# First batch of a fused attention and MoE kernel: the last 64 rows of k, v and phi as one 128-partition transfer each

## The chip, the core and the metric

The kernel runs on one core of one Trainium2 chip. The metric is the device time of one execution in microseconds (us): 696.65 us is the median of three runs before the change (696.21 to 697.31). Engines are named as the profile names them: PE multiplies matrices (PEld loads its stationary operand), DVE is the vector engine, ACT the scalar engine, POOL the general-purpose engine, SP the sync engine, which issues most transfers. SPq and ACTq are the two queues on which transfers are issued; 16 DMA engines, shared by both queues, move the bytes.

## What is computed

```python
a = exp(phi - max(phi, axis=2)); a = a / (sum(a, axis=2) + 1e-9)      # over 32 memory slots
k_m = einsum('bhsm,bhsd->bhmd', a, k); v_m = einsum('bhsm,bhsd->bhmd', a, v)
scores = q @ k_m.T / sqrt(64)
attn = softmax(scores); out = attn @ v_m                              # per head
x = out.transpose(0, 2, 1, 3).reshape(4608, 512)
h = relu(x @ w_in); return (h * h) @ w_out                            # 512 -> 2048 -> 512
```

There are 8 batches, 8 heads, 576 positions, 64 values per head and 32 memory slots; everything is float32. The sequence of 576 positions is four full chunks of 128 rows and a last one of 64 rows. The sum over slots in `a` is divided out after the products over positions have been made.

## The kernel before, in words

The heads go in two *quads* of four heads. For one batch, `e_sb` holds phi with positions on the partitions: five chunks of 128 x 256 values, where the first 128 columns are quad 0 and the last 128 quad 1. `exp_phi` takes the largest value over the five chunks (`phi_mx`, lines 186 and 189), turns that with PE (206), reduces it (209), broadcasts it with PE (214), adds it on DVE (224) and exponentiates on ACT (225), chunk by chunk. `memories` then makes, chunk by chunk and quad by quad, the sums of the exponentials (`add`, line 318) and their products with k and v (`product`, line 327); between chunk 1 and chunk 2, after the sums of chunk 2, two dummy products stand (line 341). Lines 382 to 391 and 417 divide, turn and store the memories (`mem`). `attend` makes scores from q and `mem` (439) and the softmax on DVE and ACT (466 to 493). `decode` (lines 584 to 609) turns the 64-bit words in which the weights arrive into float32, partly on ACT, partly on DVE, last on POOL or DVE. Then follow the two MoE products, which fill the rest of the time.

What runs ahead of the steady stage is written out by hand. `loads` is the list of transfers in order; the first 12 entries are issued before any computation of the program is written, the others after it. `order` is the list in which the steps of the first batch are written, and so the order in which each engine's own instructions stand:

```python
order = (
    "e e e e e m d0 m m d0 m d1 a0 a0 a0 d0 a0 d1 d2 d1 a0 d2 u0 s a1 u0 d2 a0 o0 m o0"
)
```

Here `e` is a step of `exp_phi`, `m` of `memories`, `d0`, `d1` and `d2` of decoding w_in, `a0` and `a1` of `attend`, `u0` of the product of w_in with the memories, `o0` of decoding w_out. So the first DVE step of `d0` (lines 594 and 597) stands on DVE ahead of the copy that stores `mem` (line 417).

Transfers take eight semaphores in turn, in the order in which the program issues them on both queues together, and each transfer waits on its queue until the one eight places earlier has landed. The transfers of the first microseconds are: on ACTq the last 64 rows of phi (line 168), then three of quad 0's k and v (`u_hi`, `u_lo` at line 1316 with 256 rows each, `u_hi` at line 1320 with the last 64 rows); on SPq phi's chunks 0 and 1 (174), chunks 2 and 3 (176), three of quad 1's k and v (`wp` at 1316 twice and at 1320), then the first piece of w_in (565), q in two halves (428), and weights.

Of the kernel before, what the change touches and what calls it, by code (L numbers as in the profile page):

```python
# [9 lines left out]
F32 = mybir.dt.float32  # L10
# [17 lines left out]
def attn_moe_kernel(ctx: ExitStack, tc: tile.TileContext, qT, kv, phi, w_in, w_out, outT):  # L28
# [12 lines left out]
    nc = tc.nc  # L41
    ctx.enter_context(tc.manual_schedule())

    B, NQ, S = kv.shape[:3]
    P = 128
# [3 lines left out]
    D = 64  # L49
    M = 32  # L50
# [6 lines left out]
    CW = 2 * D + 2  # L57
    NCH = (S + P - 1) // P
# [9 lines left out]
    def rows(c):  # L68
        return min(P, S - c * P)

    const = ctx.enter_context(tc.tile_pool(name="const", bufs=1))
# [37 lines left out]
    e_sb = const.tile([P, NCH, NQ * P], F32, name="e_sb")  # L109
    kvb = [const.tile([P, 4, CW], F32, name=f"kvb{i}") for i in range(NCH)]  # L110

    def fill(c, t):
        if rows(c) < P:
            nc.gpsimd.memset(t[rows(c):], 0.0)
        if t.shape[-1] == CW:
            nc.gpsimd.memset(t[:rows(c), :, 2 * D:], 1.0)

    def fill_all():
        for c in range(NCH):
            fill(c, kvb[c])  # L120
            if rows(c) < P:
                nc.gpsimd.memset(e_sb[rows(c):, c], 0.0)

    ones = const.tile([P, CW - 2 * D], F32, name="ones")
    nc.gpsimd.memset(ones, 1.0)
# [35 lines left out]
    def load_phi(b, nc_q=nc.sync):  # L161
        nfull = S // P
        assert b == 0 or ("products", b - 1) in ready
        n = nfull if b else nfull // 2
        x = phi[b, :nfull * P].rearrange("(c p) x -> p c x", p=P)
        def short():
            if nfull < NCH:
                nc_q.dma_start(out=e_sb[:rows(nfull), nfull], in_=phi[b, nfull * P:])
                if b >= 3:
                    nc_q.dma_start(out=e_sb[P - rows(nfull):, nfull], in_=phi[b, nfull * P:])  # L170

        if not b:
            short()
        nc.sync.dma_start(out=e_sb[:, :n], in_=x[:, :n])
        if not b:
            nc.sync.dma_start(out=e_sb[:, n:nfull], in_=x[:, n:])
        if b:
            short()
        return [e_sb[:P if b >= 3 else rows(c), c] for c in range(NCH)]

    def chunk_max(e):

# [119 lines left out]
    def memories(b, e, kvs, mem):  # L302
# [9 lines left out]
        accs = [bank(ps, qd if not b or two else 0)[:, (qd if b and not two else 0) * CW:] for qd in range(NQ)]  # L312
        sums = [(ps_h.tile([P, 512], F32, name="h") if qd else tp) if not b else accs[qd][:, 2 * D:] for qd in range(NQ)]

        def add(qd, c):
            n = kvs[qd][c].shape[0]
            for j in range(4):
                nc.tensor.matmul(
                    sums[qd][M * j:M * (j + 1), :CW - 2 * D], e[c][:n, qd * P + M * j:qd * P + M * (j + 1)], ones[:n],
                    start=(c == 0), stop=(c == len(kvs[qd]) - 1),  # L320
                )

        def product(qd, c):
            y = kvs[qd][c]
            n, w = y.shape[0], y.shape[-1]
            for j in range(4):
                nc.tensor.matmul(  # L327
                    accs[qd][M * j:M * (j + 1), :w],
                    e[c][:n, qd * P + M * j:qd * P + M * (j + 1)],
                    y[:, j, :], start=(c == 0), stop=(c == len(kvs[qd]) - 1),  # L330
                )

        turns = range(NQ)
        if not b:
            for c in range(NCH):
                for qd in turns:
                    add(qd, c)
                if c == 2:
                    idle = new_ps(True)
                    for _ in range(2):  # L340
                        nc.tensor.matmul(
                            bank(idle, 0), ident, ident[:, None, :].broadcast_to([P, 4, P]), start=True, stop=True
                        )
                    done_ps(idle)
                for qd in turns:
                    product(qd, c)
        for qd in turns if b else ():
            if kvs[qd][0].shape[-1] < CW:
                for c in range(len(kvs[qd])):
                    add(qd, c)  # L350
            for c in range(NCH - 1 if two or whole else NCH):
                product(qd, c)
            if whole:
                for j in range(4):
                    nc.tensor.matmul(
                        accs[qd][M * j:M * (j + 1), :CW], e_sb[:, NCH - 1, qd * P + M * j:qd * P + M * (j + 1)],
                        kvb[NCH - 1][:, j, :], start=False, stop=True,
                    )
        if two:
            n = rows(NCH - 1)  # L360
            for j in range(4):
                for qd in range(NQ):
                    y = kvs[qd][-1] if qd else kvs[qd][-1][:n]
# [22 lines left out]
        for qd in turns:  # L386
            x = accs[qd][:, :2 * D].rearrange("p (x d) -> p x d", x=2)[:, :, None, :].broadcast_to([P, 2, 2, D])
# [9 lines left out]
        if b > 2:  # L397
            done_ps(ps)
            for j in range(4):
                if j == 2 or j and b > JOIN:  # L400
                    yield
                for k in range(2):
                    for x in range(2):
                        at = M * (2 * (j % 2) + k)
# [775 lines left out]
    def from_z(j, k, name, bufs):  # L1180

        x = work.tile([P, T], F32, name=name, bufs=bufs)
        (nc.vector.tensor_copy if late_on[f"z{k}"] >> pairs[j][1] & 1 else nc.scalar.copy)(x, banks["z"][:, :T])  # L1183
        return x
# [30 lines left out]
    def task_phi(b):  # L1215
        state[b]["phi"] = load_phi(b)
# [9 lines left out]
    def task_mem(b, kvs=None):  # L1226
        kvs = kvs or [state[b]["kv"][qd] for qd in range(NQ)]
        new_mem(b)
        return memories(b, [e_sb[:, c] for c in range(NCH)], kvs, state[b]["mem"])
# [68 lines left out]

    st = state[0]
    kvs = [None] * NQ  # L1300

    def first_kv(qd):

        if qd:
            x = [const.tile([P, 2, 2, 4, 2 * D], F32, name=f"wp{k}") for k in (2, 3)]
            rooms = [x[0][:, 0], x[0][:, 1], x[1][:, 0]]
        else:
            rooms = [const.tile([P, 2, 4, 2 * D], F32, name=n) for n in ("u_hi3", "u_lo3", "u_hi4")]
        queues = ((nc.scalar, nc.scalar, nc.scalar), (nc.sync, nc.sync, nc.sync))[qd]
        got = []  # L1310
        for t, nc_q in zip(rooms, queues):
            c = len(got)
            n = min(2, S // P - c)
            if n:
                x = kv[0, qd, c * P:(c + n) * P].rearrange("(c p) h x -> p c h x", p=P)
                nc_q.dma_start(out=t[:, :n], in_=x)
                got += [t[:, k] for k in range(n)]
            else:
                fill(c, t[:, 0])
                nc_q.dma_start(out=t[:rows(c), 0], in_=kv[0, qd, c * P:])  # L1320
                got.append(t[:, 0])
        kvs[qd] = got

    def first_phi():
        st["phi"] = load_phi(0, nc.scalar)
        fill_all()

    def next_kv():
        state[1]["kv"][1] = load_kv(1, 1, in_u())

    loads = [
        (first_phi,),
        (first_kv, 1),
        (fetch_w_in, 0, 0),
        (task_q, 0, 0),
        (fetch_w_in, 0, 1),
        (fetch_w_in, 1, 1),
        (fetch_w_in, 1, 0),
        (fetch_w_out, 0),
        (first_kv, 0),  # L1340
        (fetch_w_out, 1),
        (task_q, 0, 1),
# [215 lines left out]
    for k, step in enumerate(steps):  # L1558
        i, b, t, f = step
# [5 lines left out]
        n = f * P // FC  # L1565
# [53 lines left out]
    for j in range(-1, LAST + 1):  # L1619
# [31 lines left out]
        if new:  # L1651
            ffn1_product(u1, j + 1, 1, True)
            ffn1_product(z, j + 1, 2, True)
            x = from_z(j + 1, 2, *(("g_hi", 3) if old else ("r", 2)))
# [19 lines left out]
    n = (B - JOIN) * REST  # L1674
# [23 lines left out]
    last = banks["h"] + [banks["z"], banks["m"]]  # L1698
# [55 lines left out]
```

## Time and profile before

| | |
|---|---|
| median of three runs | 696.65 us |
| the profiled execution's own time | 695.58 us |
| its span, first to last instruction | 693.5 us |
| PE busy in the span | 682.5 us (98%) |
| PE busy in 0 to 45 us | 38.0 us of 45 |

The profiled execution is 1.07 us under the median, and 2.08 us of its time lie outside the span. PE busy in the first 45 us is the sum of nine stretches of 5 us. A busy PE is not PE at its peak, because matmuls are pipelined and dummy products count as busy. In the rows, "idle before <- X" is the time that an engine waited and what ended the wait; a wait for several semaphores is put down to the one that came last.

### The profile page before, as it was taken

How to read it: one execution, taken by the hardware profiler on the slowest of the kernel's cores; microseconds unless marked ns; L12 is line 12 of the kernel's file. 1: busy time of each engine (PE TensorE's matmuls, PEld its weight loads, DVE VectorE, ACT ScalarE, POOL GpSimd, SP SyncE). 2: the span in 40 equal slices, each digit the busy share in tenths (PEclk: the TensorE clock that was granted, in tenths of full speed). 3: DMA queues.
4: the chain of work that ended last, by engine and by line, in shares of the span. 5: the costliest groups of instructions: out<-in, count | busy, mean ns of one | idle time of the engine just before them, and what ended most of it. 6: DMA issues, size and time to landing. Idle time of an engine off the chain costs nothing.

```text
span 693.5 us, 14173 instructions
## 1 busy us (share of the span) xinstructions
PE 682.5 (98%) x5102; PEld 573.8 (83%) x5102; DVE 480.5 (69%) x1132; ACT 439.7 (63%) x1193; POOL 345.0 (50%) x528
## 2 busy tenths in 40 slices
PE   8899999999999999999999999999999999999997
PEld 4367889899998888888888888888888888888897
DVE  3879849455787976788678976788677765564432
ACT  3867798876456675566666665667666575655531
POOL 2200343343367675747575675757585567554200
PEclk9999999999999999999999999999999999999999
DMA  9997352509424642082336243355106110400102
GB/s 304 353 376 263 126 163 60 187 2 268 139 62 147 219 129 100 25 251 86 97 116 210 88 130 122 118 180 151 64 18 211 62 60 4 166 17 1 57 6 46
DMA packets 67846, 89.85 MB, mean 130 GB/s; under 512 B 6848, under 2 KB 56064, under 8 KB 64192
## 3 DMA queue, kind: packets, MB, share of 16 engines
q1 hardware_dynamic: 65888, 87.41, 38.9%
q10 hardware_dynamic: 1888, 1.54, 0.7%
q8 instruction: 40, 0.66, 0.4%
q14 instruction: 30, 0.25, 0.1%
HBM read 75.30 MB, written 13.63 MB: 128 GB/s over the span
## 4 chain that ended last, share of the span: by engine, by line
PE 91%; DMA 6%; DVE 2%; ACT 1%; issue 0%; ACTq 0%; SPq 0%; DVEq 0%
PE acc L1112 39%; PE h L1136 11%; PE acc L716 9%; PE z L1136 8%; PE h L687 6%; PE acc L708 4%; PE h L1704 2%; DMA e_sb<-in_phi 1%; DMA u_lo<-in_kv 1%; PE z L448 1%; PE m L1704 1%; PE z L1704 1%; PE ps_m L439 1%; PE m L327 1%; PE m L448 1%; DMA wp<-in_w_in 1%
## 5 line engine op out<-in xcount | busy, mean ns | idle before, releaser
L1112 PE MATMUL acc<-u_hi,wp 128*128 128x512 f32 x576 | 153.8, 396 | 0.0
L1112 PE MATMUL acc<-u_lo,wp 128*128 128x512 f32 x576 | 140.0, 392 | 0.0
L1112 PEld LDWEIGHTS acc<-u_hi,wp 128*128 128x128 f32 x576 | 101.2, 188 | 25.9 <-issue 11.0
L1112 PEld LDWEIGHTS acc<-u_lo,wp 128*128 128x128 f32 x576 | 105.5, 188 | 20.5
L1160 POOL TENSOR_TENSOR u_hi<-g_lo,u_hi 128x288 fp32r<-128x288 f32 (+1 forms) x76 | 59.2, 779 | 64.1 <-ACT g_lo L1157 44.2
L700 POOL TENSOR_TENSOR g_lo<-g,g_hi 128x288 fp32r<-128x288 f32 x48 | 43.2, 901 | 78.1 <-ACT g_hi L698 51.4
L1016 POOL TENSOR_TENSOR u_lo<-low,u_hi 128x128 fp32r<-128x128 f32 (+1 forms) x116 | 73.2, 636 | 16.6 <-ACT u_hi L1015 16.0
L1015 ACT CAST u_hi<-low 128x256 fp32r<-128x256 f32 (+1 forms) x160 | 52.8, 347 | 23.0 <-POOL low L1027 19.0
L1152 DVE CUSTOM_DVE_ANT_0 g_hi<-h,g_hi 128x288 f32<-128x288 f32 x95 | 42.7, 449 | 24.5 <-ACT g_hi L1183 24.2
L716 PE MATMUL acc<-g_hi,wp 128*128 128x288 f32 x360 | 58.8, 297 | 0.0
L1183 ACT COPY g_hi<-z 128x288 f32<-128x288 f32 x72 | 28.6, 398 | 44.2 <-PE z L1136 36.6
L716 PEld LDWEIGHTS acc<-g_hi,wp 128*128 128x128 f32 x360 | 51.0, 188 | 4.4 <-ACT r L689 1.7
L1155 ACT ACTIVATE u_hi<-g_hi 128x224 fp32r<-128x224 f32 x95 | 39.0, 410 | 21.7 <-DVE g_hi L1152 21.7
L1177 DVE TENSOR_TENSOR g_lo<-h,g 128x288 f32<-128x288 f32 x48 | 21.5, 448 | 34.9 <-ACT g L1173 33.8
L689 ACT ACTIVATE r<-h 128x288 f32<-128x288 f32 x64 | 26.0, 406 | 27.9 <-PE h L687 27.6
L1136 PE MATMUL z<-a_hi,u_hi 128*128 128x288 f32 x120 | 35.3, 294 | 0.0
L1136 PE MATMUL h<-a_lo,u_hi 128*128 128x288 f32 x120 | 34.6, 295 | 0.0
L716 PE MATMUL acc<-g_lo,wp 128*128 128x288 f32 x180 | 34.6, 295 | 0.0
L1178 POOL TENSOR_TENSOR u_lo<-g_lo,u_lo 128x288 fp32r<-128x288 f32 x30 | 25.1, 835 | 18.5 <-DVE g_lo L1177 18.5
L708 PE MATMUL acc<-g_hi,wp 128*128 128x288 f32 x128 | 33.7, 410 | 0.5 <-ACT a_hi L508 0.5
L1136 PE MATMUL h<-w_sb,u_hi 128*128 128x288 f32 x120 | 34.1, 296 | 0.0
L687 PE MATMUL h<-a_hi,u_hi 128*128 128x288 f32 x128 | 30.8, 327 | 1.0 <-DVE a_hi L493 1.0
(374 smaller groups left out, 1778.1 us busy)
## 6 DMA issues: line engine op xcount, KB each, us to landing
w_sb<-w_f SPq DMA_DIRECT2D x24, 1024.0 KB, 5.5
wp<-in_w_in SPq DMA_DIRECT2D x16, 512.0 KB, 8.4
wp<-in_w_out SPq DMA_DIRECT2D x16, 512.0 KB, 7.9
kvb<-in_kv SPq DMA_DIRECT2D x28, 256.0 KB, 7.1
tmp<-in_kv SPq DMA_DIRECT2D x24, 256.0 KB, 5.8
q_sb<-in_q SPq DMA_DIRECT2D x15, 384.0 KB, 4.7
w_f<-w_sb SPq DMA_DIRECT2D x4, 1024.0 KB, 6.4
e_sb<-in_phi SPq DMA_DIRECT2D x7, 512.0 KB, 4.2
```

The source lines that it names most:

```text
L687: nc.tensor.matmul(h[:, :T], u[:, qd, fs], x[:, qd], start=(i == 0), stop=(i == len(todo) - 1))
L700: nc.gpsimd.tensor_tensor(out=g_lo, in0=g, in1=g_hi.bitcast(F32), op=ALU.subtract)
L708: nc.tensor.matmul(acc[e][:, :T], wo[f][:, e * P:(e + 1) * P], g_hi, start=first, stop=last)
L716: nc.tensor.matmul(acc[e][:, :T], wo[f][:, w, e * P:(e + 1) * P], x, start=first and x is g_hi and w == 0, stop=last and x is g_lo,)
L1015: nc.scalar.copy(hi[:, k], x)
L1016: by(name, p).tensor_tensor(out=lo[:, k], in0=x, in1=hi[:, k].bitcast(F32), op=ALU.subtract)
L1112: nc.tensor.matmul(late_accs[e], wo[f][:, w, e * P:(e + 1) * P], x, start=f == 0 and first, stop=f == NFT - 1 and last,)
L1136: nc.tensor.matmul(out[:, :T], u[:, lhs], a, start=first and not n, stop=n == 2, skip_group_check=not first)
L1152: nc.vector._custom_dve(TENSOR_ADD_SAT, out=x, in0=u[:, :T], in1=x, s0=float("inf"), s1=0.0)
L1155: nc.scalar.square(g_hi, x[:, :n])
L1160: by(f"c{k}", p).tensor_tensor(out=g_lo, in0=g[:, :n], in1=g_hi.bitcast(F32), op=ALU.subtract)
L1183: (nc.vector.tensor_copy if late_on[f"z{k}"] >> pairs[j][1] & 1 else nc.scalar.copy)(x, banks["z"][:, :T])
```

## The change

For batch 0 only, the last 64 rows are loaded otherwise:

- phi's last 64 rows are loaded twice in one transfer, into partitions 0 to 63 and again into 64 to 127 of chunk 4. The source is a view with a repeated outer dimension, 2 x 64 rows x 256 values; the target is 128 rows. It stays on ACTq as the first issue.
- The last 64 rows of k and v of both quads come in one transfer on SPq into 128 partitions of one tile: quad 0 in partitions 0 to 63, quad 1 in 64 to 127. The source is a view of 2 quads x 64 rows x 512 values. The separate transfer of quad 0 on ACTq is gone.
- In `memories`, quad 1's sums and products of chunk 4 read partitions 64 to 127 of `e_sb`, of the loaded tile and of `ones`; quad 0's read 0 to 63 as before.
- `phi_mx`, the addition of the maximum and the exponential of chunk 4 work on 128 partitions in place of 64.
- Three memsets of POOL leave the start: the lower halves of the two k and v tiles go, and that of `e_sb` moves to the loads of batch 1.

```diff
@@ load_phi
-            if nfull < NCH:
+            if nfull < NCH and not b:
+                n = rows(nfull)
+                y = phi[b:b + 1, nfull * P:].broadcast_to([P // n, n, NQ * P])
+                nc_q.dma_start(out=e_sb[:, nfull], in_=y)
+            elif nfull < NCH:
+                if b == 1:
+                    nc.gpsimd.memset(e_sb[rows(nfull):, nfull], 0.0)
                 nc_q.dma_start(out=e_sb[:rows(nfull), nfull], in_=phi[b, nfull * P:])
...
-        return [e_sb[:P if b >= 3 else rows(c), c] for c in range(NCH)]
+        return [e_sb[:P if b >= 3 or not b else rows(c), c] for c in range(NCH)]
@@ memories
+        def part(qd, c):
+            n = kvs[qd][c].shape[0]
+            at = P - n if not b and qd else 0
+            return slice(at, at + n)
...
-                    e[c][:n, qd * P + M * j:qd * P + M * (j + 1)],
+                    e[c][n, qd * P + M * j:qd * P + M * (j + 1)],
@@ first_kv
+        if qd:
+            n = S - 4 * P
+            nc_q.dma_start(out=last, in_=kv[0, :, 4 * P:])
+            ends.extend([last[:n], last[P - n:]])
```

On SP, at the program's start (`wp` is quad 1's k and v at first, then weights; `DMAHW0` to `DMAHW7` are the eight semaphores), the queue stands so before:

```order
L174 DMA e_sb<-in_phi 128x2x256
L176 DMA e_sb<-in_phi 128x2x256
L1316 DMA wp_108<-in_kv 128x2x512 x2
L1320 DMA wp_109<-in_kv 64x512 [waits DMAHW0_49]
L565 DMA wp_114<-in_w_in 128x512 [waits DMAHW1_49]
L428 DMA q_sb<-in_q 128x2x288 [waits DMAHW2_49]
L428 DMA q_sb<-in_q 128x2x288 [waits DMAHW3_49]
L565 DMA wp_114<-in_w_in 128x512 [waits DMAHW4_49]
```

and so after:

```order
L178 DMA e_sb<-in_phi 128x2x256
L180 DMA e_sb<-in_phi 128x2x256
L1324 DMA wp_107<-in_kv 128x2x512 x2
L1329 DMA wp_108<-in_kv 128x1x512
L574 DMA wp_112<-in_w_in 128x512 [waits DMAHW0_49]
L437 DMA q_sb<-in_q 128x2x288 [waits DMAHW1_49]
L437 DMA q_sb<-in_q 128x2x288 [waits DMAHW2_49]
L574 DMA wp_112<-in_w_in 128x512 [waits DMAHW3_49]
```

The order is the same; the last transfer of k and v no longer waits, the first piece of w_in waits for phi's last rows in its place, and each of the next loads waits for a transfer one place earlier than before.

On ACT, at the same place (`u_hi` and `u_lo` are quad 0's k and v), before:

```order
L168 DMA e_sb<-in_phi 64x256
L1316 DMA u_hi_125<-in_kv 128x2x512
L1316 DMA u_lo_126<-in_kv 128x2x512
L1320 DMA u_hi_127<-in_kv 64x512
L1363 ACT_TABLE_LOAD
```

and after:

```order
L168 DMA e_sb<-in_phi 128x1x256
L1324 DMA u_hi_123<-in_kv 128x2x512
L1324 DMA u_lo_124<-in_kv 128x2x512
L1374 ACT_TABLE_LOAD
L1374 ACTIVATE ones<-ones 1x1 [waits Pool_49]
```

One issue is gone, and the first writes 128 rows. No instruction of PE or DVE changes its place.

## Rows read from the trace of the kernel before

**Rows 1.** The page: span, busy time and share of each engine.

```profile
span 693.5 us, 14173 instructions
PE 682.5 (98%) x5102; PEld 573.8 (83%) x5102; DVE 480.5 (69%) x1132; ACT 439.7 (63%) x1193; POOL 345.0 (50%) x528
```

**Rows 2.** Windows: busy time by engine, then PE clock, DMA share, GB/s.

```profile
45.00:50.00 5.00, 5.00 (x37) 3.38 (x36) 2.62 (x4) 2.98 (x9) 0.00 (x0) 1.00 1.06 409
```

**Rows 3.** Timeline of DVE, first 21 us: start, duration, instruction, idle before.

```profile
4.78 1.34 DVE L189 TENSOR_TENSOR phi_mx<-phi_mx,e_sb 128x256 f32<-128x256 f32 x3 [0.58 <-DMA e_sb<-in_phi]
...
14.68 0.88 DVE L388 TENSOR_SCALAR st<-acc,den 128x256 f32<-128x256 f32 x2
15.47 0.42 DVE L594 TENSOR_SCALAR tmp<-tmp 128x512 f32<-128x512 f32 x1
15.93 0.43 DVE L597 TENSOR_SCALAR tmp<-tmp 128x512 int32<-128x512 int32 x1
16.27 0.41 DVE L417 COPY mem<-h 64x256 f32<-64x256 f32 x1
18.03 0.85 DVE L466 STREAM_TRANSPOSE st<-acc 128x288 f32<-128x288 f32 x2 [1.36 <-PE acc L439]
```

**Rows 4.** Timeline of all engines: the PE instructions of the first batch.

```profile
1.35 5.49 PE L159 MATMUL h<-ident 128*128 128x512 f32 x6 [1.35 <-POOL tiny L128]
...
10.87 1.98 PE L341 MATMUL ps_m<-ident 128*128 128x512 f32 x4
...
13.93 0.40 PE L327 MATMUL acc<-u_hi,e_sb 128*32 128x128 f32 x8
...
16.73 1.27 PE L439 MATMUL acc<-q_sb,mem 64*32 64x288 f32 x16 [0.68 <-DVE mem L417]
```

**Rows 5.** Transfers issued in 0 to 30 us: KB each, median us to landing.

```profile
DMA packets 5280, 10.09 MB, mean 336 GB/s; under 512 B 397, under 2 KB 2859, under 8 KB 5278
...
wp<-in_kv SPq DMA_DIRECT2D x1, 128.0 KB, 8.6
...
e_sb<-in_phi ACTq DMA_DIRECT2D x1, 64.0 KB, 3.4
```

**Rows 6.** Timeline of ACT and its queue, first 21 us.

```profile
0.73 0.57 ACTq L168 DMA_DIRECT2D e_sb<-in_phi  x1
...
13.82 0.70 ACT L584 ACTIVATE tmp<-wp 128x512 f32<-128x512 f32 x1 [3.11 <-DMA wp<-in_w_in]
...
17.91 0.66 ACT L584 ACTIVATE tmp<-wp 128x512 f32<-128x512 f32 x1 [0.83 <-DMA wp<-in_w_in]
...
19.16 0.87 ACT L590 ACTIVATE low<-wp,tiny 128x512 f16<-128x512 f32 x1
20.50 0.69 ACT L478 ACTIVATE st<-st 128x576 f32<-128x576 f32 x1 [0.47 <-DVE st L476]
```

**Rows 7.** Windows of half a microsecond, columns as in Rows 2.

```profile
8.50:9.00 0.50, 0.50 (x2) 0.03 (x1) 0.47 (x2) 0.01 (x1) 0.00 (x0) 1.00 1.01 389
9.50:10.00 0.50, 0.50 (x31) 0.50 (x35) 0.50 (x3) 0.50 (x3) 0.00 (x0) 1.00 1.08 246
17.00:17.50 0.50, 0.50 (x16) 0.18 (x14) 0.00 (x0) 0.08 (x1) 0.50 (x1) 1.00 1.09 434
17.50:18.00 0.50, 0.50 (x15) 0.07 (x1) 0.00 (x0) 0.09 (x1) 0.30 (x1) 0.55 0.99 393
```

**Rows 8.** Transfers issued at 0.74 us: phi's chunks 0 and 1.

```profile
e_sb<-in_phi SPq DMA_DIRECT2D x1, 256.0 KB, 3.0
```

**Rows 9.** Timeline of all engines: the last k and v of batch 1.

```profile
33.92 0.50 SPq L298 DMA_DIRECT2D u_hi<-in_kv  x1
...
43.36 0.43 PE L327 MATMUL ps_m<-u_hi,e_sb 128*32 128x128 f32 x8
```

**Rows 10.** Transfers issued at 33.9 us.

```profile
u_hi<-in_kv SPq DMA_DIRECT2D x1, 128.0 KB, 6.6
```

**Rows 11.** Timeline of POOL.

```profile
31.03 1.41 POOL L510 TENSOR_TENSOR a_lo<-a_hi,a_hi 128x576 fp32r<-128x576 f32 x1 [7.77 <-ACT a_hi L508]
```

More of the change, by code (lines that the diff above doesn't have):

```diff
@@ L120, in fill_all @@
             fill(c, kvb[c])
-            if rows(c) < P:
-                nc.gpsimd.memset(e_sb[rows(c):, c], 0.0)
     ones = const.tile([P, CW - 2 * D], F32, name="ones")
@@ L313, in memories @@
         sums = [(ps_h.tile([P, 512], F32, name="h") if qd else tp) if not b else accs[qd][:, 2 * D:] for qd in range(NQ)]
+        def part(qd, c):
+            n = kvs[qd][c].shape[0]
+            at = P - n if not b and qd else 0
+            return slice(at, at + n)
         def add(qd, c):
-            n = kvs[qd][c].shape[0]
+            n = part(qd, c)
             for j in range(4):
                 nc.tensor.matmul(
-                    sums[qd][M * j:M * (j + 1), :CW - 2 * D], e[c][:n, qd * P + M * j:qd * P + M * (j + 1)], ones[:n],
+                    sums[qd][M * j:M * (j + 1), :CW - 2 * D], e[c][n, qd * P + M * j:qd * P + M * (j + 1)], ones[n],
                     start=(c == 0), stop=(c == len(kvs[qd]) - 1),
@@ L324, in product @@
             y = kvs[qd][c]
-            n, w = y.shape[0], y.shape[-1]
+            n, w = part(qd, c), y.shape[-1]
             for j in range(4):
@@ L1300, in attn_moe_kernel @@
     kvs = [None] * NQ
+    ends = []
     def first_kv(qd):
@@ L1305, in first_kv @@
             x = [const.tile([P, 2, 2, 4, 2 * D], F32, name=f"wp{k}") for k in (2, 3)]
-            rooms = [x[0][:, 0], x[0][:, 1], x[1][:, 0]]
-        else:
-            rooms = [const.tile([P, 2, 4, 2 * D], F32, name=n) for n in ("u_hi3", "u_lo3", "u_hi4")]
-        queues = ((nc.scalar, nc.scalar, nc.scalar), (nc.sync, nc.sync, nc.sync))[qd]
+            rooms = [x[0][:, 0], x[0][:, 1]]
+            last = x[1][:, 0, 0]
+        else:
+            rooms = [const.tile([P, 2, 4, 2 * D], F32, name=n) for n in ("u_hi3", "u_lo3")]
+        nc_q = nc.sync if qd else nc.scalar
         got = []
-        for t, nc_q in zip(rooms, queues):
+        for t in rooms:
             c = len(got)
[L1313 to L1321, printed above, removed]
-        kvs[qd] = got
+            nc_q.dma_start(out=t, in_=kv[0, qd, c * P:(c + 2) * P].rearrange("(c p) h x -> p c h x", p=P))
+            got += [t[:, k] for k in range(2)]
+        kvs[qd] = got
+        if qd:
+            n = S - 4 * P
+            nc_q.dma_start(out=last, in_=kv[0, :, 4 * P:])
+            ends.extend([last[:n], last[P - n:]])
+        if len(ends) == NQ and kvs[0] and kvs[1]:
+            for q in range(NQ):
+                kvs[q].append(ends[q])
     def first_phi():
```

## The prediction

> **What bounds the kernel now.** I read the page first: PE is busy for 98% of the span [rows 1]. The windows say where the rest is: from 45 us on PE has no gap worth the name [rows 2], and before that it is busy for 38.0 of 45 us. So the time is the start plus a steady stage that the change does not touch, and a shift of the start goes through to the end one for one. What matters is which wait ends last in the first 45 us.
>
> The timeline of DVE gives that chain. The maximum over phi waits 0.58 us for phi's chunks 2 and 3 and starts again at 4.78; its three steps last 1.34 us, so the third, which needs phi's last 64 rows, starts at about 5.67 and ends at 6.12 [rows 3]. Then PE, DVE and ACT follow each other up to the products with k and v. The two dummy products hold PE from 10.87 to 12.85; chunk 4's products start at 13.93, and the scores at 16.73 [rows 4]. Between the two stand, in DVE's own order, the scaling by the sums (14.68), the first decoding step d0 (15.47 and 15.93) and the copy that stores mem (16.27); DVE goes on with the scores at 18.03 [rows 3]. So chunk 4 and d0 both stand ahead of everything that follows, and each waits for a load: phi's rows and those of k and v, and the first piece of w_in.
>
> No load is late in the profile. Phi's last rows land 3.4 us after their issue at 0.73, at 4.1, and k and v's last rows of quad 1 8.6 us after 4.10, at 12.7 [rows 5, 6]: 1.5 us and 1.2 us before they are wanted. ACT starts on the first piece of w_in as it lands, at 13.82, and is done with the part that DVE needs at 14.52, 0.95 us before DVE's turn at 15.47 [rows 3, 6].
>
> **The change part by part.** *One transfer fewer.* One ACTq issue goes; ACT has nothing to do until phi has come, so nothing is gained there. With one place fewer among the eight semaphores, seven loads from k and v's last rows on wait for an earlier transfer, and w_in's second piece no longer waits for u_lo. Nothing on the chain waited for these: that piece comes at 17.91, its three ACT steps end at 20.03, and the exponential behind them starts only at 20.50, released by DVE [rows 6]. Gain 0.
>
> *DVE and ACT.* Chunk 4 has 128 partitions in place of 64, at the same 256 columns; DVE's three maxima take 1.34 us together, two of 128 and one of 64 partitions, so 0.45 us each whatever the partitions [rows 3]. Cost 0. *PE*: quad 1's chunk 4 stands in the other half of the array's rows, so the two quads may overlap; one quad's products take 0.40 us [rows 4], so the gain is at most that and is bounded by DVE, which starts its scaling only at 14.68. I take 0.
>
> *Two transfers with an outer dimension of 2.* This is the term that decides. The source of the new phi transfer is 2 x 64 rows, that of the new k and v transfer 2 x 64 rows; every transfer in the program before starts with a dimension of 64 or more. No row shows how one with 2 blocks is dealt to the 16 DMA engines. One end is as all others, to all 16: then phi's 128 KB in place of 64 KB move in the time of 64 KB more, 0.17 us at 389 GB/s, and the price is 0 to 0.2 us. The other end is one block to one engine: two engines carry all 128 KB and all 256 KB, beside their sixteenth of every other load. I take the second end; nothing but the shape speaks for it in the trace, so the first stays a rival with its own chance.
>
> The Trainium skill, on the page "DMA: Bandwidth & Descriptors", section "Why a DMA increments its semaphore by 16 and not by 1", says that the number of engines is the largest one up to 16 that divides the slowest dimension of both access patterns, and its rules for authors warn of a leading zero-stride broadcast; by that both transfers get two engines. No run shown here has such a transfer, and no number below is taken from that page.
>
> The price, by rows. All 16 engines together move 389 GB/s when nothing holds them [rows 7], 24.3 GB/s or 23.7 KB/us for each. The first phi load of SP lands 3.0 us after its issue [rows 8]; its 256 KB and the 64 KB beside it take 0.84 us of that, so about 2.2 us are fixed, and an engine that is never idle has moved n KB by 0.73 + 2.2 + n / 23.7.
> - Phi's last rows: 64 KB on each of two engines. If SP's queue gets as many bytes there in that time, 128 KB, landing at 2.93 + 5.4 = 8.3 against 5.67 wanted: +2.6 us. If the engine did them first, 64 KB, 5.6: no delay. If row for row with SP's, whose rows of k and v are twice as long (64 + 16 + 16 + 32 + 32 = 160 KB), 9.7: +4.0.
> - The last rows of k and v: behind all of that on the same two engines. 64 (phi) + 32 (chunks 0 to 3) + 64 (u_hi, u_lo) + 64 (two wp) + 128 = 352 KB, landing at 2.93 + 14.9 = 17.8, against 13.93: +3.9 us. This is not on top of the first term but takes its place.
> - The first piece of w_in, next in the queue: 384 KB, 2.93 + 16.2 = 19.1. ACT's 0.70 us bring DVE's d0 to 19.85 against 15.47: **+4.4 us**. Again the longer one counts, not the sum.
> - w_in's second piece: 36 KB of q and 32 KB more, 22.0; with ACT's 2.12 us 24.1, against the exponential at 20.50 + 4.4 = 24.9. Hidden, with 0.8 us to spare.
> - Further on the two engines lag by what they carry too much: 192 KB in place of 20 for the same rows, 172 / 23.7 = 7.3 us. The chain itself is 4.4 us later, so loads may lose 2.9 us against it. The tightest that I found is the last of batch 1's k and v: issued 33.92, landing 6.6 us later at 40.5, used at 43.36, a cover of 2.8 us [rows 9, 10]. Just hidden; without that cover up to 1 us more.
> - PE's clock: in the first batch the granted clock falls from 1.00 to 0.55 in the mean of 17.5 to 18.0, from the level of 2.4 to that of 1.2 GHz, after PE had been idle for parts of 14.5 to 16.7, and the scores take 1.27 us [rows 4, 7]. With longer gaps in the same place it falls earlier and more of them runs at the lower level; I put 0.3 us on it.
>
> *POOL.* Three memsets leave the start, where POOL then idles; that of e_sb comes in before batch 1's, and POOL waits 7.77 us afterwards [rows 11]. 0.
>
> Sum: 4.4 + 0.3 = +4.7 us. Against the profiled execution 695.58 + 4.7 = 700.3; against the median, 1.07 us above that execution, **701.3 us**.
>
> **Rivals.** *A. All 16 engines take their part* (not slower). Then phi's last rows land at about 4.2 and those of k and v earlier than 12.7, since they no longer wait for phi's landing at 4.1. The rate falls to 246 GB/s at 9.5 us, where 64-row transfers are under way [rows 7]; filling that brings later loads forward by under 1 us, but no engine on the chain waits for them. 696.6 us, give or take 0.4. It decides on one point: whether phi's last rows land by 5.67 and those of k and v by 13.9. For it: every load of the trace spreads. Against: its shape is unlike all of these.
>
> *B. Two engines, and PE's clock falls during the first products.* PE's dummy products end at 6.84 [rows 4]; with phi at 8.3 PE idles for 2 us there, as long as before the fall at 17.5. If the 3.4 us of work from 9.5 to 12.85 then ran at half speed, chunk 2 would start at 12.85 + 2.6 + 3.4 = 18.9, and the chain would be 6.0 us late in place of 4.4: 702.9 us.
>
> *C. Two engines at another rate.* The highest rate of the trace is 434 GB/s [rows 7], 26.5 KB/us for one engine: w_in at 17.4, d0 +2.7, 699.3 us. The mean over the first 30 us is 336 GB/s [rows 5], 20.5 KB/us: w_in at 21.7, d0 +6.9, 703.6 us; with 1 us of late loads in batch 1, 704.6.
>
> *D. Two engines, but hidden.* Only if phi went first and one engine could be much faster alone than a sixteenth of the whole; ends at 384 KB by 15 us would need 32 KB/us. I give it no more than a part of the low end.
>
> **How the numbers follow.** A measurement of this kernel can tell 0.2%, 1.4 us, from no change. Two engines (forecast, B, C): 0.83, of which the forecast with C's inner half 0.50, B 0.18, C's ends 0.15. All of them are slower by over 1.4 us but 0.01: slower 0.82. A and D give the same: 0.15. Faster: 0.03, for a gain of A's loads in a place that I do not see. The range 698.9 to 704.6 goes from C's fast end to its slow end with late loads; it holds about 0.8, and A lies outside it.
>
> **What would show it.** Right: phi's last rows land at 8 us or later, not at 4.2; those of k and v at 16 to 20; the windows from 8 to 17 us show a DMA rate well under 389 GB/s, because 14 engines run dry while SPq waits for the landings; DVE's third maximum waits 2 to 4 us for a load; ACT's first decoding starts at 17 to 22 in place of 13.82; the scores start at 19.5 to 24. From 50 us on the two profiles are alike but for the shift. Wrong: phi's last rows landing near 4.2 (then A), a start of the scores later than 24 (then lags or the clock were undersized), or gaps of PE after 45 us.

## The result, and the profile after

| | before | after |
|---|---|---|
| median of five runs | 696.21 us (694.95 to 697.31) | 701.51 us (701.39 to 702.02) |
| the profiled execution's own time | 695.58 us | 701.51 us |
| its span | 693.5 us | 699.4 us |

The ratio is 1.0077, 95% interval 1.0062 to 1.0092: the change costs 5.3 us. The forecast was 701.3 us, slower.

The page of after, busy time and share of each engine, then all packets (under them the line on packets of the page of before):

```profile
span 699.4 us, 14167 instructions
PE 683.5 (98%) x5102; PEld 574.3 (82%) x5102; DVE 480.6 (69%) x1132; ACT 439.6 (63%) x1193; POOL 343.7 (49%) x526
...
DMA packets 67866, 89.91 MB, mean 129 GB/s; under 512 B 6804, under 2 KB 56084, under 8 KB 64212
```

```profile
DMA packets 67846, 89.85 MB, mean 130 GB/s; under 512 B 6848, under 2 KB 56064, under 8 KB 64192
```

The work is as it was: PE is busy for 1.0 us more than before in a span that is 5.9 us longer [rows 1]. Two POOL instructions are gone. The packets under 512 bytes are 44 fewer, which is used below.

The timeline of DVE in after (start, duration, instruction, idle before):

```profile
6.60 0.88 DVE L193 TENSOR_TENSOR phi_mx<-phi_mx,e_sb 128x256 f32<-128x256 f32 x2 [2.52 <-DMA e_sb<-in_phi]
9.29 0.43 DVE L193 TENSOR_TENSOR phi_mx<-phi_mx,e_sb 128x256 f32<-128x256 f32 x1 [1.81 <-DMA e_sb<-in_phi]
...
20.25 0.88 DVE L397 TENSOR_SCALAR st<-acc,den 128x256 f32<-128x256 f32 x2 [0.90 <-PE acc L336]
21.56 0.43 DVE L603 TENSOR_SCALAR tmp<-tmp 128x512 f32<-128x512 f32 x1 [0.43 <-ACT tmp L593]
...
22.36 0.41 DVE L426 COPY mem<-h 64x256 f32<-64x256 f32 x1
24.78 0.85 DVE L475 STREAM_TRANSPOSE st<-acc 128x288 f32<-128x288 f32 x2 [2.00 <-PE acc L448]
```

The three maxima, one row before [rows 3], are two rows now. The first two wait 2.52 us for phi's chunks 2 and 3, and the last one 1.81 us more for phi's last rows. Further down the scaling (L397, 388 before) and d0 (L603, 594 before), which waited for nothing, wait for PE and for ACT.

The timeline of PE in after:

```profile
9.77 0.69 PE L210 MATMUL acc<-ident,phi_mx 128*128 128x128 f32 x2 [4.09 <-DVE phi_mx L193]
...
19.76 0.45 PE L336 MATMUL acc<-wp,e_sb 64*32 64x128 f32 x16 [0.90 <-DMA wp<-in_kv]
...
22.83 1.87 PE L448 MATMUL acc<-q_sb,mem 64*32 64x288 f32 x16 [1.16 <-DVE mem L426]
...
50.12 0.43 PE L336 MATMUL ps_m<-u_hi,e_sb 128*32 128x128 f32 x8
```

Chunk 4's products now wait for k and v's last rows, and start as these land. The scores take 1.87 us, 1.27 before [rows 4]. ACT's decoding, and on SP's queue the issues of k and v's last rows and of the load that ACT waits for:

```profile
20.85 0.68 ACT L593 ACTIVATE tmp<-wp 128x512 f32<-128x512 f32 x1 [6.42 <-DMA wp<-in_w_in]
```

```profile
2.75 0.69 SPq L1329 DMA_DIRECT2D wp<-in_kv  x1
9.21 0.35 SPq L574 DMA_DIRECT2D wp<-in_w_in  x1
```

The first piece of w_in comes at 20.85, 13.82 before [rows 6]. Put side by side, how late each step is:

| step | before | after | later by | forecast |
|---|---|---|---|---|
| third maximum | 5.67 | 9.29 | 3.6 | 2.6 (bound 4.0) |
| chunk 4's products | 13.93 | 19.76 | 5.8 | 3.9 |
| d0 on DVE | 15.47 | 21.56 | 6.1 | 4.4 |
| scores on PE | 16.73 | 22.83 | 6.1 | 4.4 |
| scores read by DVE | 18.03 | 24.78 | 6.75 | 4.7 |
| batch 1's last products | 43.36 | 50.12 | 6.76 | 4.7 |
| end of the span | 693.5 | 699.4 | 5.9 | 4.7 |

From 25 to 50 us nothing more is lost; between 100 us and the end some 0.9 us come back. Windows show part of that: PE idles for 0.26 us between 100 and 400 us in before and not at all in after. Before, then after:

```profile
100.00:200.00 100.00, 99.92 (x921) 93.28 (x921) 64.24 (x114) 70.72 (x146) 39.54 (x53) 1.00 0.45 133
200.00:400.00 200.00, 199.82 (x1481) 168.99 (x1483) 161.41 (x424) 126.89 (x386) 132.71 (x206) 1.00 0.40 129
```

```profile
100.00:200.00 100.00, 100.00 (x869) 93.04 (x868) 63.29 (x96) 74.27 (x149) 38.76 (x53) 1.00 0.47 136
200.00:400.00 200.00, 200.00 (x1543) 170.18 (x1543) 161.36 (x432) 125.07 (x379) 131.80 (x204) 1.00 0.43 133
```

Product by product, PE of after is 6.76 us behind up to 134 us, 6.33 us from 136 us and 6.00 us from 223 us on. At the last of these steps PE of before waits for DVE, and the same product of after follows without a wait (before first):

```profile
222.58 0.40 PE L1136 MATMUL z<-w_sb,u_hi 128*128 128x288 f32 x1 [0.18 <-DVE g L1183]
```

```profile
228.58 0.41 PE L1145 MATMUL z<-w_sb,u_hi 128*128 128x288 f32 x1
```

The medians, 5.3 us apart, are somewhat nearer than the two profiled executions.

### The profile page after: what moved, and what is told of

The parts are those of the page before. It is cut to its first block, busy times and chain, and to the rows that moved or that the text cites. A ratio compares the mean times of both kernels' runs of the same rounds, so it can differ in the third digit from the quotient of the medians.

```text
span 699.4 us, 14167 instructions
## 1 busy us (share of the span) xinstructions
PE 683.5 (98%) x5102; PEld 574.3 (82%) x5102; DVE 480.6 (69%) x1132; ACT 439.6 (63%) x1193; POOL 343.7 (49%) x526
## 2 busy tenths in 40 slices
DMA packets 67866, 89.91 MB, mean 129 GB/s; under 512 B 6804, under 2 KB 56084, under 8 KB 64212
## 4 chain that ended last, share of the span: by engine, by line
PE 93%; DMA 4%; DVE 1%; ACT 1%; ACTq 0%; SPq 0%; issue 0%
PE acc L1121 38%; PE h L1145 11%; PE acc L725 10%; PE z L1145 8%; PE h L696 7%; PE acc L717 4%; PE h L1715 2%; DMA wp<-in_w_out 2%; DMA u_lo<-in_kv 2%; PE ps_m L448 1%; PE z L457 1%; PE m L1715 1%; PE z L1715 1%; PE m L336 1%; PE m L457 1%; PE ps_m L336 1%
## 5 line engine op out<-in xcount | busy, mean ns | idle before, releaser
L1121 PEld LDWEIGHTS acc<-u_lo,wp 128*128 128x128 f32 x576 | 105.5, 188 | 20.5
L1164 ACT ACTIVATE u_hi<-g_hi 128x224 fp32r<-128x224 f32 x95 | 39.0, 411 | 21.7 <-DVE g_hi L1161 21.7
```

What stands on the lines that cost most here:

```text
L1121: nc.tensor.matmul(late_accs[e], wo[f][:, w, e * P:(e + 1) * P], x, start=f == 0 and first, stop=f == NFT - 1 and last,)
L1164: nc.scalar.square(g_hi, x[:, :n])
```

## The experiments

The theory is that an outermost dimension of 2 puts a whole transfer on two engines. The rivals: merging itself or chunk 4 on 128 partitions costs the time, whatever the engines (M); one of the two transfers does all the harm (O); PE's clock does part of it (B).

**Each transfer cut in two, and each kept whole with the rows outermost.** `both_in_two` differs from after in both loads:

```diff
-                y = phi[b:b + 1, nfull * P:].broadcast_to([P // n, n, NQ * P])
-                nc_q.dma_start(out=e_sb[:, nfull], in_=y)
+                for i in range(P // n):
+                    nc_q.dma_start(out=e_sb[i * n:(i + 1) * n, nfull], in_=phi[b, nfull * P:])
...
-            nc_q.dma_start(out=last, in_=kv[0, :, 4 * P:])
+            for q in range(NQ):
+                nc_q.dma_start(out=last[q * n:(q + 1) * n], in_=kv[0, q, 4 * P:])
```

> The changed kernel, but phi's last rows and those of k and v come in two transfers of 64 rows each, into the same partitions. Two-engine theory: each transfer again has 64 rows as its outermost dimension, so phi's last rows land at about 4.2 to 4.6 us, the third maximum of DVE starts at 5.7 as before the change, the copy of mem at 16.3, and the time is that of the kernel before, ratio 0.999 to 1.001. Rival theory (the wider work costs: 128 partitions of chunk 4, the new order of the loads, the moved memset): all of that is still there, so 1.006 to 1.009.

`rows_outermost` keeps one transfer each, with the same bytes to the same tiles, and exchanges the two outer dimensions of the source, so that the rows land in other partitions. The products of the last 64 rows then mix the two quads; the kernel leaves out what would keep them apart.

```diff
-                y = phi[b:b + 1, nfull * P:].broadcast_to([P // n, n, NQ * P])
+                y = phi[b, nfull * P:].rearrange("s (o x) -> s o x", o=1).broadcast_to([n, P // n, NQ * P])
...
-            nc_q.dma_start(out=last, in_=kv[0, :, 4 * P:])
+            nc_q.dma_start(out=last, in_=kv[0, :, 4 * P:].rearrange("q s h x -> s q h x"))
```

> The changed kernel, both transfers still single, of the same bytes and into the same 128 partitions, but the source view has the 64 rows outermost and the 2 copies (or quads) inside, so that row r goes to partitions 2r and 2r+1. The products of the last 64 rows then mix the two quads: this run leaves that part of the computation out of order. Two-engine theory: outermost dimension 64, so as before the change: phi's last rows by 4.6 us, ratio 0.999 to 1.001. Rival (one transfer for two blocks, or reading a row twice, is slow whatever the order): 1.006 to 1.009, phi's last rows at 9 us.

Measured, on one chip (times are medians; the ratios are not quotients of these medians): rows_outermost 695.32 us, ratio to before 0.9989 (0.9979 to 0.9998); both_in_two 697.41 us, 1.0022 (1.0010 to 1.0033). So M falls: with 64 outermost the merged transfers cost nothing. both_in_two lost 1.5 us where none was expected. Its PE timeline has the reason:

```profile
10.91 0.43 PE L336 MATMUL acc<-u_hi,e_sb 128*32 128x128 f32 x8 [1.41 <-DMA u_hi<-in_kv]
...
14.61 0.42 PE L336 MATMUL acc<-u_lo,e_sb 128*32 128x128 f32 x8 [0.47 <-DMA u_lo<-in_kv]
```

Quad 0's k and v wait behind two phi transfers on ACTq and come 1.9 us too late in all.

**Each of the two alone.** `phi_in_two` has the first half of that diff, so that only k and v go with 2 outermost; `kv_in_two` the second half, so that only phi does.

> The changed kernel with phi's last rows in two transfers of 64 rows; k and v's last rows stay one transfer. Two-engine theory: phi in time; the two engines carry 296 KB until k and v's last rows are there, which at the 20.8 KB/us that the changed kernel's landings give is 17.1 us, against 13.9 wanted; w_in's first piece at 18.7, DVE's first decoding step at 19.5 in place of 15.5: +3.5 to +5.0 us, ratio 1.005 to 1.007. Rival (the late phi alone makes the loss, through the chain behind it): 1.000.

> The changed kernel with k and v's last rows in two transfers of 64 rows; phi's stay one transfer. Two-engine theory: phi's last rows at 9.2 us as in the changed kernel, DVE's third maximum 3.6 us late, PE's clock falls in the gap and the first products are 4.7 to 4.9 us late; k and v's rows at 14.5 and w_in at 16 are no longer late behind that, so +4.0 to +4.9 us in all, ratio 1.0055 to 1.007. The two losses stand for one another and do not add: this run and the one with phi in two together cost more than the changed kernel's 5.3 us. Rival (they add): the two runs' losses sum to 5.3 us.

Measured: phi_in_two 701.64 us, 1.0082 (1.0064 to 1.0100), a loss of 5.7 us where 3.5 to 5.0 were expected; kv_in_two 700.19 us, 1.0055 (1.0038 to 1.0072), 4.3 us, as expected. So O falls too: either alone makes most or all of the loss, and they don't add. The intervals do not tell the 5.7 us from the 5.3 of after. PE of phi_in_two, and SP and ACT with the first piece of w_in:

```profile
16.13 0.27 PE L327 MATMUL h<-ones,e_sb 64*32 64x2 f32 x16
20.10 0.68 PE L336 MATMUL acc<-wp,e_sb 64*32 64x128 f32 x16 [3.70 <-DMA wp<-in_kv]
```

```profile
5.06 2.28 SPq L574 DMA_DIRECT2D wp<-in_w_in  x1
```

```profile
21.11 0.67 ACT L593 ACTIVATE tmp<-wp 128x512 f32<-128x512 f32 x1 [9.73 <-DMA wp<-in_w_in]
```

PE is ready for chunk 4 at 16.40 and waits 3.70 us; in after, where phi is late as well, it waits only 0.90 us, and both start within 0.4 us of each other. The delay of phi is swallowed by that of k and v. The row of SP settles another doubt: in after w_in's first piece is issued at 9.21, because it waits for phi's landing, and one could blame that. Here its issue starts at 5.06 and it comes no sooner. What fits is that its own share on the two engines stands behind k and v; the profile does not show single engines, so this step is inferred.

**2, 4 and 16 outermost, in the kernel before.** The three 64-row transfers of before keep their rows, places and queues, and only the order of the rows in the transfer changes (`a` = 2, 4 or 16):

```diff
-                nc_q.dma_start(out=e_sb[:rows(nfull), nfull], in_=phi[b, nfull * P:])
+                y = phi[b, nfull * P:]
+                if not b:
+                    y = y.rearrange("(r a) x -> a r x", a=2)
+                nc_q.dma_start(out=e_sb[:rows(nfull), nfull], in_=y)
...
-                nc_q.dma_start(out=t[:rows(c), 0], in_=kv[0, qd, c * P:])
+                nc_q.dma_start(out=t[:rows(c), 0], in_=kv[0, qd, c * P:].rearrange("(r a) h x -> a r h x", a=2))
```

> The kernel before, where the three transfers of last rows (phi, and k and v of each quad: 64, 128 and 128 KB as before, 64 partitions as before) take their rows in another order, even rows and then odd ones, so that the source's outermost dimension is 2; phi and k and v in the same order, so that the result is the same. Two-engine theory: phi's chunks 2 and 3 at about 6.0 in place of 4.8, k and v's last rows near 18, w_in's first piece near 20, DVE's first decoding step at 20.6 in place of 15.5: +4 to +6 us, ratio 1.006 to 1.0085. Rival (doubled bytes, 128 partitions or the changed queue cost, not the outermost dimension): 0.999 to 1.001.

> As the run with the outermost dimension of 2, with every fourth row first, so that it is 4. Theory that the outermost dimension sets the number of engines: four engines with half the surplus each; phi 0.4 us late, w_in's first piece near 16.5 to 17, +1.0 to +2.5 us, ratio 1.0015 to 1.0035. Rival (any source that is not in row order is slow): as with 2.

> As the run with the outermost dimension of 2, with every sixteenth row first, so that it is 16. Theory of the outermost dimension: all 16 engines take part, as before, ratio 0.999 to 1.001. Rival (rows out of order are slow): as with 2.

Measured, on one chip: 701.30 us, 1.0080 (1.0065 to 1.0095) with 2; 699.17 us, 1.0049 (1.0034 to 1.0063) with 4, a loss of 3.2 us where 1.0 to 2.5 were expected; 695.54 us, 1.0000 (0.9987 to 1.0013) with 16, where the rows are out of order too. Nothing of the change is in these kernels but the shape, and it makes the whole loss. Half-microsecond windows of before_outer_2, in which PE waits for k and v's last rows (columns as in [rows 2]), and PE's wait:

```profile
17.00:17.50 0.50, 0.00 (x0) 0.00 (x0) 0.00 (x0) 0.00 (x0) 0.00 (x0) 1.00 1.04 283
...
18.50:19.00 0.50, 0.00 (x0) 0.00 (x0) 0.00 (x0) 0.00 (x0) 0.00 (x0) 0.93 0.19 74
19.00:19.50 0.50, 0.00 (x0) 0.00 (x0) 0.00 (x0) 0.00 (x0) 0.00 (x0) 0.50 0.13 47
19.50:20.00 0.50, 0.13 (x4) 0.16 (x8) 0.00 (x0) 0.00 (x0) 0.00 (x0) 0.50 0.14 48
20.00:20.50 0.50, 0.50 (x13) 0.50 (x15) 0.00 (x0) 0.47 (x1) 0.00 (x0) 0.50 0.14 48
```

```profile
19.87 0.65 PE L330 MATMUL acc<-u_hi,e_sb 128*32 128x128 f32 x8 [3.65 <-DMA u_hi<-in_kv]
```

Here two engines stand alone in the picture. From 19.0 to 20.5 us the DMA share is 0.13 to 0.14, that is 2 of 16, and they move 47 to 48 GB/s, 24 GB/s each. The other fourteen have run dry.

**Counting the engines.** Packets under 512 bytes, from the line on packets of each page. If every engine that takes part in a transfer leaves one small packet, then before has 48 from its three transfers and 6800 from all others, and the rest must follow:

| kernel | transfers and engines | 6800 and | page |
|---|---|---|---|
| before, before_outer_16 | 3 on 16 | 48 | 6848, 6848 |
| after | 2 on 2 | 4 | 6804 |
| both_in_two | 4 on 16 | 64 | 6864 |
| rows_outermost | 2 on 16 | 32 | 6832 |
| phi_in_two, kv_in_two | 2 on 16, 1 on 2 | 34 | 6834, 6834 |
| before_outer_2 | 3 on 2 | 6 | 6806 |
| before_outer_4 | 3 on 4 | 12 | 6812 |

All agree to the packet, and so do the three kernels further down: 6834 in kv_in_two_spin, 6832 in rows_masked, 6864 in copy_on_sp. The Trainium skill, on the page "DMA: Bandwidth & Descriptors", section "Why a DMA increments its semaphore by 16 and not by 1", says that every engine of a transfer counts its own end on the semaphore, and that their number is the largest up to 16 that divides the outermost dimensions; the counts and the times here agree for 2, 4, 16 and 64.

**The clock.** `kv_in_two_spin` is kv_in_two with seven in place of three dummy products at the start, so that PE isn't idle while phi is late:

```diff
-    spin(3, ident)
+    spin(7, ident)
```

> The changed kernel with k and v's last rows in two transfers (as in the run of that name), and seven dummy products of PE at the start in place of three, which reach to the time at which phi's maximum is there. Theory that the fall of PE's clock in the gap costs about 1.2 us behind the late phi: 1.0 to 1.4 us less than the run without them. Rival (the clock's fall is hidden behind later waits): the same as that run within 0.3 us.

Measured: 698.27 us, 1.0038 (1.0023 to 1.0053), a loss of 2.3 us in place of kv_in_two's 4.3. The two ran on different chips, where before took 695.99 and 695.91 us. Windows of 2 us, kv_in_two and then kv_in_two_spin:

```profile
10.00:12.00 2.00, 1.48 (x6) 1.33 (x6) 0.49 (x2) 0.00 (x0) 0.00 (x0) 0.50 1.00 257
12.00:14.00 2.00, 2.00 (x25) 0.48 (x28) 1.68 (x5) 1.61 (x5) 0.00 (x0) 0.50 0.84 262
```

```profile
10.00:12.00 2.00, 1.57 (x6) 0.74 (x6) 1.20 (x4) 0.37 (x2) 0.00 (x0) 1.00 1.05 265
12.00:14.00 2.00, 1.85 (x81) 1.77 (x82) 0.92 (x3) 1.37 (x5) 0.00 (x0) 1.00 0.86 249
```

The granted clock is 0.50, the level of 1.2 GHz, after PE had been idle, and 1.00 where the dummies filled that. The loss is 2.0 us smaller than in kv_in_two, where 1.0 to 1.4 were expected. With four runs of each on two chips the size is uncertain by some 1.5 us, but the traces agree: the third maximum starts at 8.99 in both, and DVE reads the scores 2.5 us earlier with the dummies (kv_in_two first):

```profile
23.31 0.85 DVE L475 STREAM_TRANSPOSE st<-acc 128x288 f32<-128x288 f32 x2 [1.40 <-PE acc L448]
```

```profile
20.79 0.85 DVE L475 STREAM_TRANSPOSE st<-acc 128x288 f32<-128x288 f32 x2 [1.25 <-PE acc L448]
```

So of the 4.3 us that phi alone costs, about 2.0 are clock and 2.3 the wait itself.

**Versions that might win.** `rows_masked` takes rows_outermost's transfers; the exponential of chunk 4 zeroes, in each quad's columns, the partitions of the other quad, and the products run over all 128:

```diff
+    nc.vector.tensor_reduce(out=away, in_=ident.rearrange("p (x t) -> p t x", t=NQ), axis=AX.X, op=ALU.max)
+    nc.vector.tensor_scalar(out=away, in0=away, scalar1=-1.0, scalar2=1000.0, op0=ALU.add, op1=ALU.mult)
...
+            for qd in range(NQ):
+                x = e[4][:, qd * P:(qd + 1) * P]
+                nc.scalar.activation(x, x, AF.Exp, bias=away[:, qd:qd + 1])
```

> The 64 rows outermost in both transfers, as in rows_outermost, but with the right result: partition 2r holds row r of quad 0, 2r+1 that of quad 1; the exponential of chunk 4 is made per quad with a bias of -1000 on the other quad's partitions, so that they become zero, and both quads' products run over all 128 partitions. Two-engine theory: both transfers get 16 engines, so no load is late; ratio to before 0.998 to 1.0005. What it adds (two small DVE steps while DVE waits for phi, one more exponential of half width on ACT) should be hidden, since chunk 4's exponential in rows_outermost is done 2 us before its sums. If merging by itself cost something, whatever the engines, it would be 1.002 or more. Small-packet count as in rows_outermost, 6832.

`copy_on_sp` is both_in_two with phi's second copy issued on SP:

```diff
+            nc.sync.dma_start(out=e_sb[rows(nfull):, nfull], in_=phi[b, nfull * P:])
```

> both_in_two with the second copy of phi's last rows issued on SP behind phi's other chunks in place of on ACT's queue ahead of quad 0's k and v. In both_in_two PE waited 1.41 us for quad 0's first k and v, issued at 1.96 in place of 1.34 and behind 64 KB more of phi. If that issue place is the whole of its 1.5 us, the ratio comes back to 0.998 to 1.001; if the extra bytes or transfers are to blame wherever they stand, it stays at 1.002 or more.

Measured, on one chip: rows_masked 694.55 us, 0.9991 (0.9983 to 1.0000); copy_on_sp 697.67 us, 1.0037 (1.0024 to 1.0050). The first is inside the 0.2% that counts as no change: its store of mem starts at 15.85 against 16.27 [rows 3], so some 0.4 us of gain is what the trace supports. The second does not come back to the time of before. Quad 0's k and v came in time, but DVE:

```profile
7.52 0.42 DVE L193 TENSOR_TENSOR phi_mx<-phi_mx,e_sb 128x256 f32<-128x256 f32 x1 [1.45 <-DMA e_sb<-in_phi]
```

Behind SP's phi chunks the copy lands 1.45 us too late for the third maximum, and PE's granted clock is 0.55 in the mean of 10 to 12 us behind that gap. So the one transfer more has a price in both places that were tried.

The Trainium skill, same page, section "Rules for kernel authors", says that two transfers into two halves of the partitions bring nothing over one into 128. On the chip of the first runs one transfer with 64 outermost took 695.32 us and two halves 697.41, so the runs agree. The section gives as its reason that both halves spread over all 16 engines; the one transfer with 2 outermost does not, and after took 701.51 us.

## Why the prediction was right, and where its sizes were off

*What bounds the kernel.* Right. The loss is made before 25 us, and 5.9 of 6.76 us go through to the end.

*Two transfers with an outer dimension of 2.* Right, and it is the whole change: packet counts, the windows with 2 of 16 engines and the three shapes in the kernel before show it. Rival A, all 16 engines, is out, and so is D, two engines without a loss.

*Which wait decides.* Right as a pattern, that the waits take each other's place: phi_in_two and kv_in_two lose 5.7 and 4.3 us, after 5.3. The forecast let d0 decide, behind w_in, at 4.4 us, and k and v's rows 0.5 us less. Measured, the two are 6.1 and 5.8 us late: as close, in that order.

*The price formula* is the term that was too small, by 1.7 us on d0. It gave 17.8 and 19.1 for the landings of k and v's rows and of w_in; they came at 19.76 and 20.85. With the formula's own bytes the two engines moved 352 KB in 16.83 us and 384 KB in 17.92 us after 2.93, that is 20.9 and 21.4 KB/us in place of 23.7. An engine can come close to that: before_outer_2 shows 24 GB/s, 23.4 KB/us, for one that works alone. Nor were the engines idle in the mean. Up to the landing of k and v's last rows, in before and then in after, the windows show a DMA share of about 1:

```profile
2.93:12.70 9.77, 9.11 (x97) 4.22 (x95) 3.85 (x10) 3.21 (x7) 0.64 (x2) 1.00 1.04 331
```

```profile
2.93:19.76 16.83, 11.32 (x162) 5.96 (x160) 4.29 (x13) 3.16 (x7) 0.00 (x0) 0.80 0.99 308
```

At 331 and 308 GB/s a busy engine moves 20.2 and 18.8 KB/us in the mean. So the formula took the rate of a fast half microsecond for that of the whole stretch. Why busy engines move less there, and what the two did by themselves, is not shown. The rows of before would have told: with 4 + 32 + 64 + 64 + 16 = 180 KB per engine up to quad 1's last rows the formula gives 10.5 us, and they landed at 12.7 [rows 5]. Rival C's slow end, from the mean of 336 GB/s, 20.5 KB/us, was the better size; its w_in at 21.7 was nearer than 19.1.

*Phi's last rows.* 9.29 lies between the value taken, 8.3, and the bound of 9.7 for row by row. That SP's chunks 2 and 3 come late by it, 6.60 against 4.78 for DVE's second step, was not said.

*PE's clock.* 0.3 us was put on the scores; DVE's wait for them made 0.65 us (6.1 to 6.75). Rival B's fall during the first products did happen:

```profile
8.00:10.00 2.00, 0.23 (x1) 0.23 (x2) 0.43 (x1) 0.00 (x0) 0.00 (x0) 0.50 1.03 378
10.00:12.00 2.00, 1.48 (x7) 1.08 (x7) 0.42 (x1) 0.00 (x0) 0.00 (x0) 0.50 0.94 332
12.00:14.00 2.00, 2.00 (x15) 0.49 (x16) 1.74 (x5) 1.31 (x4) 0.00 (x0) 0.50 0.95 307
14.00:16.00 2.00, 2.00 (x81) 1.79 (x78) 0.00 (x0) 0.43 (x2) 0.00 (x0) 0.85 1.04 300
```

(windows of after). In after it costs nothing, because k and v's rows end later than the slowed products; where they don't, in kv_in_two, it costs about 2.0 us. B named a real mechanism but not the one that set the end here. Its comparison was loose: before the fall at 17.5 us PE had been idle twice, for 0.67 and 0.68 us, not for 2 us.

*Costs put at nothing.* The later loads are hidden, as forecast: batch 1's last products are 6.76 us late, no more than the scores. w_in's second piece, POOL, the DVE steps of chunk 4 and the missing issue left no mark in after, and rows_outermost, which has all of them, is not slower than before. That the two quads' products may overlap is borne out: the sixteen of chunk 4 take 0.45 us in after, where those of before run from 13.93 to 14.55. As they wait for a load, nothing comes of it.

*The signs named beforehand.* Most are there. The third maximum's own wait is 1.81 us, under the 2 to 4 that were named, since the step ahead of it waits already. The windows from 8 to 17 us were to be well under 389 GB/s throughout; 378 at 8 to 10 us is not, and before itself had 246 in there [rows 7]. The reason given, that 14 engines run dry, does not show in after at all: the DMA share is 1.01 in the mean of 8 to 17 us, so the sixteen are busy in the mean, with later loads too. Dry engines show in before_outer_2, from 18 us on.

The total came out within 0.2 us of the forecast by luck, because errors of opposite sign met. The chain was 2.1 us later at 50 us than forecast and 0.9 us came back after 100 us, so the profiled executions are 5.9 us apart in place of 4.7. Against that, the forecast added 1.07 us for the distance of before's profiled execution from the median; after's lies at its median.

The range has two loose ends. Its lower bound, 698.9, lies 0.4 us under the 699.3 of C's fast end, without a step that gives it; and C's two sums leave out the 0.3 us for the clock that the forecast and B have.

## What to carry to other kernels

Before two small transfers are merged, look at the outermost dimension of the new one: with 64 outermost the merged loads were free, with 2 they held up everything that shared those two engines, and put 5.3 us on a kernel of 696. Test a formula for landings on a load of the profile at hand before it prices one that isn't there. And where several loads are late on the same path, price each landing and take the latest one; don't add.

## What the runs showed that was not expected

- Two engines alone move 47 to 48 GB/s in before_outer_2, as much for each as the 24.3 GB/s of the full load that the prediction took, and more than the 19.3 of the mean in after. So what is lost is not speed but the other fourteen.
- Four engines cost more than half of what two cost: 3.2 us against 5.3 in the kernel before.
- The time that the issue of phi's last rows takes goes by the shape, not by the bytes. With 2 outermost it is 1.13 us for 64 KB in before_outer_2 and for 128 KB in after, with 64 outermost 0.57 us for 64 KB in before [rows 6] and 0.63 for 128 KB in rows_outermost. For k and v's last rows on SP's queue the difference is small, 0.69 us in after and 0.64 in rows_outermost. The longer issue does not explain the loss: both_in_two issues quad 0's first k and v as late, at 1.96 against 1.91 in after, and loses 1.5 us. The issues of phi's last rows in after and in rows_outermost (start, duration):

```profile
0.75 1.13 ACTq L168 DMA_DIRECT2D e_sb<-in_phi  x1
```

```profile
0.74 0.63 ACTq L168 DMA_DIRECT2D e_sb<-in_phi  x1
```

- A phi that comes 3.3 us late to the third maximum (8.99 in kv_in_two) costs nearly as much again in clock as in waiting: about 2.0 and 2.3 us. Four more dummy products give the first part back.
